# Two of three block sums of a MoE1 pair kept in PSUM instead of SBUF, with one relu-and-round step from there, and a schedule replanned around it

## The chip, the core and the metric

The kernel runs on one core of a Trainium2 chip. The core has TensorE (PE, matmuls, with PEld for its weight loads), VectorE (DVE), ScalarE (ACT), GpSimd (POOL) and SyncE (SP, which here only issues DMAs). Matmuls write to PSUM, eight banks of 128 partitions x 512 fp32; the other operands lie in SBUF. The metric is the device time of one execution in microseconds (us), the median of several runs.

## The reference

Chunked attention (4 batches x 8 heads x 576 tokens, chunks of 64), then a mixture of four experts with relu (MoE1), then a gated feed-forward layer (MoE2), all in fp32:

```python
scores = scale * np.matmul(q_c, k_c.transpose(0, 1, 2, 4, 3))     # inside chunks of 64
attn = softmax(scores); x = np.matmul(attn, v_c)                  # -> x: (2304, 512)
for e in range(4):                                                # MoE1, w1 (512, 1024), w2 (1024, 512)
    out += p[:, e:e + 1] * (np.maximum(x @ w1[e], 0.0) @ w2[e])
h = out @ w_in                                                    # MoE2, w_in (512, 2048), w_out (2048, 512)
g = h * np.clip(h + 3.0, 0.0, 6.0) / 6.0
return g @ w_out
```

## The kernel before

**Tiling.** The 2304 tokens go through in three sets of 768, each set as two halves `z` of N = 384 tokens. A layer runs in groups of 512 hidden columns: eight groups `g` in MoE1 (`ph` 0) and four in MoE2 (`ph` 1). The program order of the matmuls is all of MoE1 for the three sets, then all of MoE2. A group has an **h part** (x times the first weight matrix, line L881, or L928 for the first group of each MoE1 set) and a **y part** (72 matmuls of 512 columns, L977, which multiply the activated h with the second weight matrix). Every fp32 operand is split in a rounded high part and a low part (`fp32r`), and each product is three matmuls (`HL`).

**The pair.** In all MoE1 groups but the first of each set, and in all of MoE2, the h part is computed by a scheme of seven products for a 2 x 2 block matrix (`h_pair`, called twice a group with `pr_` 0 and 1; MoE1 has 42 such pairs). The products run in the order P1, P6, P7, P5, P2, P4, P3, six matmuls of 384 columns each, into four PSUM banks of the tag `h`, called `a`, `b`, `c` and `d`: P1 and then P2 add up in `a`, P6 goes to `b`, P7 and then P4 to `c`, P5 and then P3 to `d`. VectorE forms the block sums with L891:

- `u2` = `b` + a copy of P1 (the copy is ScalarE's L898), into an SBUF tile `U`;
- `u3` = `c` + `U`, into an SBUF tile `V`; P4 waits for it, because it overwrites the bank's sum;
- `c22` = `d` + `V`, back into `V`; P3 waits for it;
- `c21` = `c` + `U` after P4, into a third SBUF tile `C`;
- `c12` = `d` + `U` after P3, back into `U`.

The fourth block, c11, is complete in bank `a` after P2.

**The gate.** Each of the four blocks then goes through `gate`, which must leave max(x, 0) as a rounded high part and a low part in a tile `gt`. For a block in PSUM (in MoE1: c11, and the plain first groups) that is two steps: ScalarE takes relu and rounds in one instruction (L951), VectorE makes max(x, 0) minus the high part (L952, its inputs one PSUM bank and one SBUF tile). For a block in SBUF (tag `c`: c22, c21 and c12) it is three: ScalarE takes relu in place (L947), ScalarE rounds (L948), VectorE subtracts (L949, both inputs in SBUF).

**PSUM.** Four banks have the tag `h`, three `y`, one `a`. The y part needs all three `y` banks. Attention of the next set is worked in between the matmuls of MoE1 in small steps (`Item`: transposes L535, scores L472, values L544), which take the `y` and `a` banks while TensorE is in an h part, and the `h` and `a` banks while it is in a y part. Its softmax runs on VectorE (L496, L501, L512, L513) and ScalarE (L505). VectorE's L512 waits for the last exponential of L505.

**What sets the order.** `Plan` lists every operation with an engine, a planned duration, a due time, its inputs and the buffers it takes, runs that list once in the kernel's own planning and then emits the instructions of every engine in the planned order. An engine takes its instructions strictly in that order, and waits where an input or a buffer is not there yet. The constants at the top (`SLACK`, `ITEMS`, `STAGES`, `LEAD`, `LOAD`, `CALM`) shift due times: of the attention steps (`ITEMS`), of the conversion of MoE2's weights, which arrive as 64-bit numbers and are converted on ScalarE, VectorE and GpSimd during MoE1 (`STAGES`), and of the weight transfers (`LEAD`, `LOAD`, `SLACK`). GpSimd splits weights (L716, L742, L825, L828) and issues the weight reloads (L767, L770).

Of the kernel before, what the change touches and what calls it, by code (L numbers as in the profile page):

```python
# [13 lines left out]
ALU = mybir.AluOpType  # L14
# [17 lines left out]
BANKS = (("hhhhh", "yahay"), ("ayaay", "yyyay"), ("ayaay", "ayaay"))
# [2 lines left out]
def raw(ap):  # L35
    return ap.bitcast(F32)
# [23 lines left out]
class Plan:  # L60
# [3 lines left out]
    LAT = 0.2  # L64
    EVERY = 0.6
    DENSE = 7.77
    CALM = 6.53
    LANES = 8

    def __init__(self, caps, filler=None, warm=0.0):  # L70
# [164 lines left out]
def fused_kernel(ctx: ExitStack, tc: tile.TileContext, q, k, v, probs, w1, w2, win, wout, out):  # L235
    nc = tc.nc
    B, H, S, D = q.shape
# [60 lines left out]
    op = plan.op  # L298
# [37 lines left out]
    for u in units:  # L336
        ph, si, g, c0, n = u
# [528 lines left out]
    def h_pair(u, pr_):  # L866
# [31 lines left out]
        cp = op("ACT", act(n), lambda: nc.scalar.copy(S(p1)(), a_()), e(0), [o["P1"]], [p1], [ps["a"]])  # L898
        u2 = op("DVE", dve(n), add(S(U), b_, S(p1)), e(1), [o["P6"], cp], [U], [ps["b"], p1])
        u3 = op("DVE", dve(n), add(S(V), c_, S(U)), e(2), [o["P7"], u2], [V], [ps["c"], U])  # L900
        c22 = op("DVE", dve(n), add(S(V), d_, S(V)), e(3), [o["P5"], u3], (), [ps["d"], V])
        product("P2", [cp])
        product("P4", [u3])
        product("P3", [c22])
        C = buf("c")
        gate(u, 2 + pr_, 1, S(V), [V], [c22], e(3, 0.5))
        gate(u, 0 + pr_, 0, a_, [ps["a"]], [o["P2"]], e(4, 0.1))
        c21 = op("DVE", dve(n), add(S(C), c_, S(U)), e(5), [o["P4"], u2], [C], [ps["c"], U])
        gate(u, 2 + pr_, 0, S(C), [C], [c21], e(5, 0.5))
        c12 = op("DVE", dve(n), add(S(U), d_, S(U)), e(6), [o["P3"], c21, u3], (), [ps["d"], U])  # L910
        gate(u, 0 + pr_, 1, S(U), [U], [c12], e(6, 0.5))

    HL = ((0, 0), (0, 1), (1, 0))

# [26 lines left out]
    def gate(u, f, z, src, bufs, after, due, n=N):  # L941
        ph, si, g, _, _ = u
        due -= soon(u)
        G = buf("gt")
        hi_, lo_ = (lambda: G.t[:, 0, :n]), (lambda: G.t[:, 1, :n])
        if ph == 0 and bufs[0].tag == "c":
            x = op("ACT", act(n), lambda: nc.scalar.activation(src(), src(), AF.Relu), due, after, (), bufs)  # L947
            hi = op("ACT", act(n), lambda: nc.scalar.copy(hi_(), src()), due + 0.1, [x], [G], bufs)  # L948
            lo = op("DVE", dve(n) * busy(ph), lambda: nc.vector.tensor_tensor(out=lo_(), in0=src(), in1=raw(hi_()), op=ALU.subtract), due + 0.3, [hi], (), [G, *bufs])  # L949
        elif ph == 0:  # L950
            hi = op("ACT", act(n), lambda: nc.scalar.activation(hi_(), src(), AF.Relu), due, after, [G], bufs)  # L951
            lo = op("DVE", dve(n), lambda: nc.vector.scalar_tensor_tensor(out=lo_(), in0=src(), scalar=0.0, in1=raw(hi_()), op0=ALU.max, op1=ALU.subtract), due + 0.3, [hi, *after], (), [G, *bufs])  # L952
        else:
            R = buf("t")
            r_ = lambda: R.t[:, :n]
            x = op("ACT", act(n), lambda: nc.scalar.activation(r_(), src(), AF.Relu, bias=half, scale=1.0 / 6.0), due, after, [R], bufs)  # L956
            x = op("DVE", dve(n), lambda: nc.vector.scalar_tensor_tensor(out=r_(), in0=r_(), scalar=1.0, in1=src(), op0=ALU.min, op1=ALU.mult), due + 0.3, [x, *after], (), [R, *bufs])  # L957
            hi = op("ACT", act(n), lambda: nc.scalar.copy(hi_(), r_()), due + 0.6, [x], [G], [R])  # L958
            lo = op("DVE", dve(n), lambda: nc.vector.tensor_tensor(out=lo_(), in0=r_(), in1=raw(hi_()), op=ALU.subtract), due + 0.9, [hi], (), [G, R])  # L959
        gts[u, f, z] = (G, lo, 0)  # L960
        return G, lo
# [239 lines left out]
```

## Time and profile before

| | |
|---|---|
| median of 3 runs (lowest, highest) | 1197.85 us (1197.01, 1198.44) |
| profiled execution, its own time | 1196.41 us |
| span of its trace | 1194.4 us |
| TensorE busy | 1175.8 us (98%) |
| VectorE, ScalarE, GpSimd busy | 731.8, 512.4, 497.2 us |
| granted TensorE clock | full in every slice of the span |

The span is the time from the first to the last instruction of the trace; the profiled execution's own time is 2.0 us longer. An engine's busy time counts its instructions, not its waits. TensorE's matmuls are pipelined, so its idle time is what is to be looked at here: the moments in which it had no matmul in flight, and what ended each of them.

### The profile page before, as it was taken

What the parts mean: (1) busy time and instruction counts of PE and PEld (TensorE: products, weight loads), DVE (VectorE), ACT (ScalarE), POOL (GpSimd) and SP (SyncE); (2) the same over time, 40 slices, a digit from 0 to 9 for tenths busy, and PEclk for the clock granted to TensorE, in tenths of its full rate; (3) what the DMA queues carried; (4) which work ended last, traced back from release to release, by engine and by line L of the source; (5) the groups of instructions that cost most, each with busy time, mean ns of one, the idle gap of its engine ahead of it and who ended that gap; (6) DMA issues with size and microseconds to landing.
All of it is one profiled execution on the core that took longest, in us unless ns stands there. A gap on an engine that the chain in (4) does not pass through costs nothing.

```text
span 1194.4 us, 19308 instructions
## 1 busy us (share of the span) xinstructions
PE 1175.8 (98%) x7028; PEld 1057.8 (89%) x7028; DVE 731.8 (61%) x1318; ACT 512.4 (43%) x1208; POOL 497.2 (42%) x569
## 2 busy tenths in 40 slices
PE   8999999999999999999999999999999999999998
PEld 7898988889989898878989999999999999989997
DVE  5656555557574776568647655758455845583555
ACT  6764545544355443444343434333323442244222
POOL 3686665641354554664365566531111111111110
PEclk9999999999999999999999999999999999999999
DMA  9788978758779997887788878966955885576651
GB/s 249 291 282 305 301 266 290 274 195 255 207 216 328 293 299 234 287 275 238 225 279 294 283 255 288 337 208 198 267 180 182 238 233 182 189 247 194 194 177 53
DMA packets 147470, 292.29 MB, mean 245 GB/s; under 512 B 69808, under 2 KB 76208, under 8 KB 147376
## 3 DMA queue, kind: packets, MB, share of 16 engines
q0 software_dynamic: 43488, 158.35, 41.7%
q1 hardware_dynamic: 102144, 131.01, 34.3%
q10 hardware_dynamic: 1744, 1.70, 0.5%
q8 instruction: 55, 0.90, 0.3%
q14 instruction: 39, 0.32, 0.1%
HBM read 213.95 MB, written 77.07 MB: 244 GB/s over the span
## 4 chain that ended last, share of the span: by engine, by line
PE 92%; DVE 3%; issue 3%; POOL 2%; DMA 1%; ACT 0%; DVEq 0%; POOLq 0%; ACTq 0%
PE y L977 47%; PE h L881 37%; PE h L928 4%; DMA k<-wp 1%; DVE c L891 1%; PE y L295 0%; POOL wp L716 0%; PE a L535 0%; DVE gt L949 0%; POOL t L742 0%; PE y L454 0%; PE h L472 0%; PE h L544 0%; PE y L544 0%; DVE wh L716 0%
## 5 line engine op out<-in xcount | busy, mean ns | idle before, releaser
L977 PE MATMUL y<-wy,gt 128*128 128x512 f32 x2592 | 602.6, 391 | 0.8 <-DVE acc L1013 0.8
L977 PEld LDWEIGHTS y<-wy,gt 128*128 128x128 f32 x2592 | 484.3, 188 | 100.4 <-DVE acc L1013 1.2
L881 PE MATMUL h<-x,wh 128*128 128x384 f32 x2772 | 492.6, 336 | 6.9 <-DVE c L891 6.5
L881 PEld LDWEIGHTS h<-x,wh 128*128 128x128 f32 x2772 | 481.1, 188 | 13.1 <-DVE c L891 9.5
L767 POOL DMA_DIRECT2D wh<-k x190 | 103.5, 546 | 210.5 <-PE h L881 181.8
L891 DVE TENSOR_TENSOR c<-h,c 128x384 f32<-128x384 f32 x264 | 145.8, 553 | 67.5 <-PE h L881 64.1
L770 POOL DMA_DIRECT2D wy<-k x112 | 61.0, 545 | 266.0 <-PE y L977 260.3
L1013 DVE SCALAR_TENSOR_TENSOR acc<-y,pn,acc 128x512 f32<-128x512 f32 x126 | 89.0, 751 | 131.2 <-PE y L977 131.2
L949 DVE TENSOR_TENSOR gt<-c,gt 128x384 fp32r<-128x384 f32 x126 | 111.0, 887 | 8.6 <-ACT gt L948 8.4
L947 ACT ACTIVATE c<-c 128x384 f32<-128x384 f32 x126 | 65.3, 525 | 101.2 <-DVE c L891 101.0
L891 DVE TENSOR_TENSOR c<-h,p 128x384 f32<-128x384 f32 x66 | 36.7, 556 | 102.5 <-PE h L881 87.6
L898 ACT COPY p<-h 128x384 f32<-128x384 f32 x66 | 31.6, 479 | 153.6 <-PE h L881 153.6
L1020 DVE TENSOR_TENSOR acc<-y,acc 128x512 f32<-128x512 f32 x53 | 36.3, 692 | 65.2 <-PE y L977 65.2
L948 ACT CAST gt<-c 128x384 fp32r<-128x384 f32 x126 | 63.4, 511 | 2.1
L956 ACT ACTIVATE t<-c,half 128x384 f32<-128x384 f32 x72 | 43.1, 613 | 38.9 <-DVE c L891 38.9
L958 ACT CAST gt<-t 128x384 fp32r<-128x384 f32 x96 | 47.0, 513 | 27.4 <-DVE t L957 27.4
L928 PE MATMUL h<-x,wh 128*128 128x384 f32 (+1 forms) x336 | 53.2, 315 | 1.0 <-DVE x L692 1.0
L928 PEld LDWEIGHTS h<-x,wh 128*128 128x128 f32 x336 | 51.4, 189 | 1.7 <-DVE x L692 1.2
L716 POOL TENSOR_TENSOR wy<-t,wy 128x512 fp32r<-128x512 f32 x32 | 41.1, 1291 | 28.0 <-ACT wy L714 25.7
L716 POOL TENSOR_TENSOR wp<-t,wp 128x512 fp32r<-128x512 f32 x32 | 41.7, 1306 | 24.6 <-ACT wp L714 24.2
L959 DVE TENSOR_TENSOR gt<-t,gt 128x384 fp32r<-128x384 f32 x96 | 50.0, 551 | 1.0
L655 ACT CAST x<-xs 128x768 fp32r<-128x768 f32 x33 | 27.0, 833 | 45.2 <-DVE xs L662 39.5
(140 smaller groups left out, 995.6 us busy)
## 6 DMA issues: line engine op xcount, KB each, us to landing
wh<-k POOLq DMA_DIRECT2D x190, 512.0 KB, 6.1
wy<-k POOLq DMA_DIRECT2D x112, 512.0 KB, 4.7
k<-wh SPq DMA_DIRECT2D x53, 512.0 KB, 3.5
k<-wp SPq DMA_DIRECT2D x44, 512.0 KB, 5.6
k<-wy SPq DMA_DIRECT2D x32, 512.0 KB, 4.6
t<-in_moe_w_dram SPq DMA_DIRECT2D x32, 256.0 KB, 4.9
w<-in_moe_w_in_dram SPq DMA_DIRECT2D x16, 512.0 KB, 5.4
w<-in_moe_w_out_dram SPq DMA_DIRECT2D x16, 512.0 KB, 5.8
```

Source lines behind the costliest of these rows:

```text
L716: return op(eng, gps(512) if eng == "POOL" else dve(512), lambda: e.tensor_tensor(out=view(b.t[:, 1]), in0=read(), in1=raw(view(b.t[:, 0]) ...
L767: wready[at_] = op("POOL", 0.6, lambda b=b, name=name: nc.gpsimd.dma_start(out=b.t, in_=kept[ph, g, name]), t - LEAD[0] + j, [stored[ph, g ...
L770: wready[key, "y", f] = op("POOL", 0.6, lambda b=b, f=f: nc.gpsimd.dma_start(out=b.t, in_=kept[ph, g, f]), t_y - LEAD[3] + n_, [stored[ph, ...
L881: nc.tensor.matmul(acc.t[:, :n], W.t[:, a, k_ * 256 + pr_ * P:k_ * 256 + (pr_ + 1) * P], X.t[:, b, k_, cs], start=new and first, stop=last ...
L891: add = lambda out, x, y: (lambda: nc.vector.tensor_tensor(out=out(), in0=x(), in1=y(), op=ALU.add))
L928: nc.tensor.matmul(ps.t[:, :m], Ws[k_ // 2].t[:, a, k_ % 2 * 256 + f % 2 * P:k_ % 2 * 256 + f % 2 * P + P], x if len(zs) == 2 else x[:, zs ...
L947: x = op("ACT", act(n), lambda: nc.scalar.activation(src(), src(), AF.Relu), due, after, (), bufs)
L948: hi = op("ACT", act(n), lambda: nc.scalar.copy(hi_(), src()), due + 0.1, [x], [G], bufs)
L949: lo = op("DVE", dve(n) * busy(ph), lambda: nc.vector.tensor_tensor(out=lo_(), in0=src(), in1=raw(hi_()), op=ALU.subtract), due + 0.3, [hi ...
L959: lo = op("DVE", dve(n), lambda: nc.vector.tensor_tensor(out=lo_(), in0=r_(), in1=raw(hi_()), op=ALU.subtract), due + 0.9, [hi], (), [G, R])
L977: nc.tensor.matmul(ps[j].t, G.t[:, a, o + j * P:o + (j + 1) * P], W.t[:, b, :], start=f == FO[0] and i == 0, stop=f == FO[-1] and i == len ...
L1013: fn = lambda: nc.vector.scalar_tensor_tensor(out=A.t, in0=ps.t, scalar=p, in1=A.t, op0=ALU.mult, op1=ALU.add)
```

## The change

Two of the three sums of a MoE1 pair no longer go to an SBUF tile. For each pair a table `BACK` says where c22, c21 and c12 are written: `p` is the PSUM bank that already took part in the sum (`b` for c22, `c` for c21), `y` a PSUM bank of the tag `y`, `s` SBUF as before. With `("pys", "pps")`, c22 goes to bank `b` in both pairs, c21 to a `y` bank in the first pair of a group and back into bank `c` in the second, and c12 stays in SBUF. Since `gate` looks at where the block lies, c22 and c21 now take its two-step way (ScalarE relu and rounding, VectorE low part). MoE2 is written as before. The planned duration of the low part that remains in SBUF is set to 0.81, and the constants of the plan are other numbers, so the whole order of MoE1 is planned anew.

```diff
-SLACK = (6.22, 4.56, 3.86, 0.88)
+SLACK = (6.85, 4.4, 5.78, 0.84)
...
-ITEMS = (48.78, 11.34, -32.4, 5.76)
-STAGES = (26.1, -30.31)
-LEAD = (12.76, 24.57, 7.4, 8.63)
-LOAD = 15.86
+ITEMS = (50.1, 19.22, -34.0, 4.11)
+STAGES = (22.53, -48.06)
+LEAD = (15.26, 27.02, 8.22, 8.26)
+LOAD = 16.23
+BACK = ("pys", "pps")
+LO = 0.81
...
-    CALM = 6.53
+    CALM = 6.55
...
-        c22 = op("DVE", dve(n), add(S(V), d_, S(V)), e(3), [o["P5"], u3], (), [ps["d"], V])
+
+
+        def goal(k_, own, there):
+            way = BACK[pr_][k_] if ph == 0 else "s"
+            if way == "p":
+                return own, []
+            if way == "s" and there is not None:
+                return there, []
+            b = buf("c" if way == "s" else "y")
+            return b, [b]
+        at22, n22 = goal(0, ps["b"], V)
+        at21, n21 = goal(1, ps["c"], None)
+        at12, n12 = goal(2, ps["d"], U)
+        c22 = op("DVE", dve(n), add(S(at22), d_, S(V)), e(3), [o["P5"], u2, u3], n22, [ps["d"], V, at22])
...
-        C = buf("c")
-        gate(u, 2 + pr_, 1, S(V), [V], [c22], e(3, 0.5))
+        gate(u, 2 + pr_, 1, S(at22), [at22], [c22], e(3, 0.5))
         gate(u, 0 + pr_, 0, a_, [ps["a"]], [o["P2"]], e(4, 0.1))
-        c21 = op("DVE", dve(n), add(S(C), c_, S(U)), e(5), [o["P4"], u2], [C], [ps["c"], U])
-        gate(u, 2 + pr_, 0, S(C), [C], [c21], e(5, 0.5))
-        c12 = op("DVE", dve(n), add(S(U), d_, S(U)), e(6), [o["P3"], c21, u3], (), [ps["d"], U])
-        gate(u, 0 + pr_, 1, S(U), [U], [c12], e(6, 0.5))
+        c21 = op("DVE", dve(n), add(S(at21), c_, S(U)), e(5), [o["P4"], u2], n21, [ps["c"], U, at21])
+        gate(u, 2 + pr_, 0, S(at21), [at21], [c21], e(5, 0.5))
+        c12 = op("DVE", dve(n), add(S(at12), d_, S(U)), e(6), [o["P3"], c21, c22, u3], n12, [ps["d"], U, at12])
+        gate(u, 0 + pr_, 1, S(at12), [at12], [c12], e(6, 0.5))
...
-            lo = op("DVE", dve(n) * busy(ph), lambda: nc.vector.tensor_tensor(out=lo_(), in0=src(), in1=raw(hi_()), op=ALU.subtract), due + 0.3, [hi], (), [G, *bufs])
+            lo = op("DVE", LO, lambda: nc.vector.tensor_tensor(out=lo_(), in0=src(), in1=raw(hi_()), op=ALU.subtract), due + 0.3, [hi], (), [G, *bufs])
```

In the pieces below the rows of the changed kernel carry its own line numbers: L893 is the block sums (L891 before), L966 the low part from PSUM (L952), L963 the low part from SBUF (L949), L961 and L962 ScalarE's two steps (L947, L948), L965 its one step (L951), and L467, L498, L503, L514 and L515 the attention's transposes and softmax steps (L465, L496, L501, L512, L513). The order of TensorE up to the end of the first h part by pairs is the same in both kernels.

**First place: VectorE in the second pair of the first paired group of the second set**, about 341 to 350 us of the trace. `c` is an SBUF tile, `h` a PSUM bank, `gt` the gate's output. Before:

```order
L949 TENSOR_TENSOR gt_4206<-c_4106,gt_4206 128x384
L891 TENSOR_TENSOR c_4218<-h_4211,c_4218 128x384
L465 STREAM_TRANSPOSE tri_78<-kr_4020 128x192
L891 TENSOR_TENSOR c_4260<-h_4193,c_4204 128x384
L949 TENSOR_TENSOR gt_4252<-c_4218,gt_4252 128x384
L952 SCALAR_TENSOR_TENSOR gt_4262<-h_4157,gt_4262 128x384
L891 TENSOR_TENSOR c_4204<-h_4211,c_4204 128x384
L949 TENSOR_TENSOR gt_4273<-c_4260,gt_4273 128x384
```

The same stretch in the changed kernel:

```order
L963 TENSOR_TENSOR gt_4169<-c_4071,gt_4169 128x384
L893 TENSOR_TENSOR c_4192<-h_4149,c_4167 128x384
L467 STREAM_TRANSPOSE tri_78<-kr_3990 128x192
L893 TENSOR_TENSOR h_4132<-h_4171,c_4192 128x384
L893 TENSOR_TENSOR h_4149<-h_4149,c_4167 128x384
L966 SCALAR_TENSOR_TENSOR gt_4203<-h_4132,gt_4203 128x384
L966 SCALAR_TENSOR_TENSOR gt_4223<-h_4123,gt_4223 128x384
L966 SCALAR_TENSOR_TENSOR gt_4228<-h_4149,gt_4228 128x384
L893 TENSOR_TENSOR c_4167<-h_4171,c_4167 128x384
```

The low parts of c22 and c21 read a PSUM bank now and stand ahead of the sum c12; the low part of the first pair's c12 (the first row of both pieces) still reads SBUF, and stands ahead of `u3` now (the second row) where it stood behind it.

**Second place: VectorE in the first pair of the fifth paired group of the first set**, about 203 to 208 us of the trace, where an attention step lies inside the h part. Before:

```order
L891 TENSOR_TENSOR c_2773<-h_2750,c_2743 128x384
L465 STREAM_TRANSPOSE tri_78<-qr_2588 128x6x32
L891 TENSOR_TENSOR c_2773<-h_2765,c_2773 128x384
L465 STREAM_TRANSPOSE tri_78<-kr_2605 128x192
L512 TENSOR_TENSOR st_2775<-st_2775,least_62 128x6
L513 RECIPROCAL st_2775<-st_2775 128x6
L465 STREAM_TRANSPOSE tri_78<-kr_2605 128x192
L891 TENSOR_TENSOR c_2824<-h_2750,c_2743 128x384
L949 TENSOR_TENSOR gt_2807<-c_2773,gt_2807 128x384
L952 SCALAR_TENSOR_TENSOR gt_2822<-h_2685,gt_2822 128x384
```

And in the changed kernel:

```order
L893 TENSOR_TENSOR c_2753<-h_2727,c_2719 128x384
L467 STREAM_TRANSPOSE tri_78<-qr_2568 128x6x32
L893 TENSOR_TENSOR h_2677<-h_2746,c_2753 128x384
L467 STREAM_TRANSPOSE tri_78<-kr_2586 128x192
L514 TENSOR_TENSOR st_2755<-st_2755,least_62 128x6
L515 RECIPROCAL st_2755<-st_2755 128x6
L467 STREAM_TRANSPOSE tri_78<-kr_2586 128x192
L966 SCALAR_TENSOR_TENSOR gt_2784<-h_2677,gt_2784 128x384
L966 SCALAR_TENSOR_TENSOR gt_2788<-h_2666,gt_2788 128x384
L893 TENSOR_TENSOR y_2812<-h_2727,c_2719 128x384
```

c22 now lies in bank `b` (`h_2677`), which stays taken until its low part, the eighth row, has read it; c21 goes to a `y` bank.

**Third place: ScalarE in the pair of the first place.** Before:

```order
L947 ACTIVATE c_4106<-c_4106 128x384
L714 CAST wp_4200<-rh_3825 128x512
L948 CAST gt_4206<-c_4106 128x384
L947 ACTIVATE c_4218<-c_4218 128x384
L948 CAST gt_4252<-c_4218 128x384
L951 ACTIVATE gt_4262<-h_4157 128x384
L947 ACTIVATE c_4260<-c_4260 128x384
L948 CAST gt_4273<-c_4260 128x384
```

And in the changed kernel:

```order
L716 CAST wp_4144<-rh_3791 128x512
L961 ACTIVATE c_4071<-c_4071 128x384
L962 CAST gt_4169<-c_4071 128x384
L965 ACTIVATE gt_4203<-h_4132 128x384
L965 ACTIVATE gt_4223<-h_4123 128x384
L965 ACTIVATE gt_4228<-h_4149 128x384
```

The two instructions of c22 and of c21 have become one each.

## Rows read from the trace of the kernel before

**Rows 1.** The page's engines: busy us (share of the span) x instructions.

```profile
PE 1175.8 (98%) x7028; PEld 1057.8 (89%) x7028; DVE 731.8 (61%) x1318; ACT 512.4 (43%) x1208; POOL 497.2 (42%) x569
```

**Rows 2.** Stretches: length, busy by engine (PE, PEld, DVE, ACT, POOL), clock, DMA share, GB/s.

```profile
0.00:66.00 66.00, 61.13 (x728) 54.24 (x729) 41.68 (x84) 46.39 (x125) 33.97 (x34) 1.00 0.86 264
66.00:650.00 584.00, 574.14 (x3589) 514.71 (x3588) 366.92 (x661) 272.30 (x714) 315.29 (x318) 1.00 0.82 266
650.00:1140.00 490.00, 490.00 (x2468) 444.30 (x2467) 295.75 (x523) 180.39 (x345) 144.24 (x212) 1.00 0.74 231
```

**Rows 3.** TensorE's waits from 66 to 650 us: total us, times, longest.

```profile
PE h L881 <- DVE c L891: 6.5, 7, 1.8
PE h L472 <- DVE gt L952: 2.2, 1, 2.2
```

**Rows 4.** Groups by line and shape: busy us, mean ns of one, idle before.

```profile
L891 DVE TENSOR_TENSOR c<-h,c 128x384 f32<-128x384 f32 x264 | 145.8, 553 | 67.5 <-PE h L881 64.1
L949 DVE TENSOR_TENSOR gt<-c,gt 128x384 fp32r<-128x384 f32 x126 | 111.0, 887 | 8.6 <-ACT gt L948 8.4
L947 ACT ACTIVATE c<-c 128x384 f32<-128x384 f32 x126 | 65.3, 525 | 101.2 <-DVE c L891 101.0
L948 ACT CAST gt<-c 128x384 fp32r<-128x384 f32 x126 | 63.4, 511 | 2.1
L952 DVE SCALAR_TENSOR_TENSOR gt<-h,gt 128x384 fp32r<-128x384 f32 x58 | 31.9, 550 | 8.5 <-ACT gt L951 8.5
L951 ACT ACTIVATE gt<-h 128x384 fp32r<-128x384 f32 x58 | 28.3, 488 | 26.2 <-PE h L928 26.0
```

**Rows 5.** The low parts line by line: ns shortest/median/longest, first and last start us.

```profile
L949 DVE TENSOR_TENSOR gt<-c,gt x126: 510/558/4062, 72.9 to 806.4; 128x384 fp32r<-128x384 f32 x126
L952 DVE SCALAR_TENSOR_TENSOR gt<-h,gt x70: 410/549/558, 29.6 to 803.3; 128x384 fp32r<-128x384 f32 x58, 128x256 fp32r<-128x256 f32 x12
L959 DVE TENSOR_TENSOR gt<-t,gt x96: 519/551/561, 825.8 to 1177.4; 128x384 fp32r<-128x384 f32 x96
```

**Rows 6.** Timeline, 344 to 350 us (start us, us): VectorE, then the TensorE step.

```profile
344.59 4.06 DVE L949 TENSOR_TENSOR gt<-c,gt 128x384 fp32r<-128x384 f32 x1
348.58 0.55 DVE L952 SCALAR_TENSOR_TENSOR gt<-h,gt 128x384 fp32r<-128x384 f32 x1
...
349.18 0.27 PE L472 MATMUL h<-tri 64*64 64x64 f32 x2 [2.16 <-DVE gt L952]
```

**Rows 7.** Timeline: VectorE's long low parts, and TensorE's waits behind them.

```profile
511.67 2.12 DVE L949 TENSOR_TENSOR gt<-c,gt 128x384 fp32r<-128x384 f32 x2
...
514.98 1.34 PE L881 MATMUL h<-x,wh 128*128 128x384 f32 x6 [1.84 <-DVE c L891]
...
546.22 1.56 DVE L949 TENSOR_TENSOR gt<-c,gt 128x384 fp32r<-128x384 f32 x1
...
548.50 0.79 PE L881 MATMUL h<-x,wh 128*128 128x384 f32 x3 [1.57 <-DVE c L891]
...
611.20 3.43 DVE L949 TENSOR_TENSOR gt<-c,gt 128x384 fp32r<-128x384 f32 x1
...
615.15 0.44 PE L881 MATMUL h<-x,wh 128*128 128x384 f32 x1 [1.34 <-DVE c L891]
```

**Rows 8.** Timeline of the second place: VectorE's L512 and c21, TensorE's matmuls.

```profile
205.70 0.17 DVE L512 TENSOR_TENSOR st<-st,least 128x6 f32<-128x6 f32 x1 [0.60 <-ACT e L505]
...
206.26 0.52 DVE L891 TENSOR_TENSOR c<-h,c 128x384 f32<-128x384 f32 x1
...
201.52 7.56 PE L881 MATMUL h<-x,wh 128*128 128x384 f32 x42
```

**Rows 9.** An undisturbed pair: TensorE's start, VectorE's c22; and an h part's length.

```profile
600.10 13.71 PE L881 MATMUL h<-x,wh 128*128 128x384 f32 x78
...
604.48 0.56 DVE L891 TENSOR_TENSOR c<-h,c 128x384 f32<-128x384 f32 x1 [0.48 <-PE h L881]
...
663.77 14.58 PE h L881 x84
```

## The prediction

> **What bounds the kernel now.** I read the page's engines first: TensorE is busy for 1175.8 of 1194.4 us, 98% [rows 1]. So the kernel is bound by its matmuls, and no change beside them can gain more than the 18.6 us in which TensorE stands still. Next I read the stretches, to see where those 18.6 us lie [rows 2]. From 0 to 66 us there are 66.00 - 61.13 = 4.9 us, in the start, where TensorE's order is the same in both kernels. From 650 to 1140 us, the last MoE1 groups and nearly all of MoE2, there is nothing: 490.00 of 490.00. The rest after 1140 us is the end of the program. What is left is MoE1 from 66 to 650 us: 584.00 - 574.14 = 9.9 us. [...] These 9.9 us are all that the change can take back.
>
> Then I read who ends TensorE's waits in that stretch [rows 3]. Seven waits, 6.5 us, are matmuls of the h part that wait for a block sum on VectorE (L891); one of 2.2 us is an attention step that waits for a low part (L952). No wait is ended by a DMA. Yet VectorE is busy for only 366.92 of the 584 us [rows 2]. It is not short of time, it is late in single places. The groups and the spread of single durations tell why [rows 4, 5]. The low part from SBUF (L949) has a median of 558 ns but a mean of 887 and a longest of 4062. The low part from PSUM (L952) never takes over 558. L949's long ones stand straight ahead of TensorE's waits: 4.06 us at 344.59, and c11's L952, which the attention step waits for, starts when it is over [rows 6]; 2.12 for two, 1.56 and 3.43 us, with waits of 1.84, 1.57 and 1.34 us behind them [rows 7]. MoE2's subtraction from two SBUF tiles (L959) stays within 561 ns [rows 5]; it stands in a stretch where GpSimd is busy for 144.24 of 490 us, against 315.29 of 584 in MoE1 [rows 2]. So my reading is that a VectorE instruction with both inputs in SBUF is held while GpSimd works on SBUF, and one with an input in PSUM is not.
>
> **The change part by part.** *Removed on ScalarE:* for c22 and c21 of 42 pairs, 84 gates, 525 + 511 ns become one step of 488 ns (L951) [rows 4]: 84 x 0.548 = 46 us of ScalarE time. All of it lies beside TensorE's work; its worth is that a low part can start 0.5 us sooner.
>
> *Removed on VectorE:* 84 x (887 - 550) ns = 28 us [rows 4], beside TensorE's work too, except where a wait stands behind it. I go through those waits. The step at 349.18 waited 2.16 us for the c22 low part of 4.06; that part now reads PSUM: 2.2 us go. At 546.22 the low part is c21's; 1.56 becomes 0.55, so 1.0 of 1.57 us goes. At 511.67 the first of two is c21's and the second c12's, which stays in SBUF and can be held in its place; I take half of 1.84, 0.9. At 611.20 it is c12's: nothing goes. What is left of 9.9 us is 9.9 - 2.2 - 1.84 - 1.57 - 1.34 = 3.0 us of smaller waits; two of three low parts are relieved there, but other VectorE work of two SBUF inputs stands in them too, so I take 1.2. Sum: 2.2 + 1.0 + 0.9 + 1.2 = 5.3 us gone.
>
> *Added: block sums written to PSUM.* No VectorE instruction of the trace writes PSUM. The nearest row is the same sum written to SBUF, 553 ns [rows 4]; a gain can't be excluded, down to the 510 ns that the shortest L949 took, and the dearest instruction of this width is L949's mean, 887 ns [rows 4, 5]. I take 553, since the work is the same and one input was in PSUM before. At 887 it would cost 0.33 us in each pair, which the margin below hides except in the seven tight pairs: 2.3 us at most.
>
> *Added: banks held longer.* This is the price of the change. Before, bank `b` was free once `u2` had read it; now it is taken until c22's low part has read it, and the second pair's first product waits for a bank. Undisturbed, c22 starts 4.38 us after its pair (604.48 - 600.10) and a pair lasts 14.58 / 2 = 7.29 us [rows 9]. Sum, relu and low part take 0.553 + 0.488 + 0.550 = 1.6 us [rows 4], so the bank is free at some 6.0 to 6.1, 1.2 us early. But VectorE works in order, and where an attention step lies in the h part, the softmax's L512 stands ahead of that low part (the second place), and it waits for ScalarE's exponentials (0.60 us) [rows 8]. The low part would stand where c21 stands now, at 206.26, and end at 206.81; the second pair's matmuls start 5 products after 201.52, at 201.52 + 30 x 14.58 / 84 = 206.73 [rows 8, 9]. That is a wait of 0.1 to 0.2 us. I count seven first pairs with those softmax steps ahead of c22's low part: 7 x 0.15 = 1.0 us.
>
> *Moved.* The attention steps inside the y part stand nine matmuls behind its start instead of six in most groups, because they need all four `h` banks; that moves them and costs no TensorE time. The weight conversion for MoE2 ends some 14 us sooner against its start (-48.06 + 30.31, with the start 3.57 earlier), so GpSimd's 315 us lie a few in a hundred denser; what hides it is VectorE's slack, and if that is gone it is c12's low part that pays. The DMA issues on SP and POOL change places by a few rows each; they cost nothing as long as no wait of TensorE is ended by a DMA, as now [rows 3]. c12's low part stands ahead of `u3` in about half of the second pairs: `u3` can start at about 3.3 us and P4 needs it at 5 x 1.04 = 5.2, so such a low part may last about 1.8 us before TensorE waits; behind `u3` it delays c22 instead, with the same room. This is the same exposure as at 611.20, for 42 low parts instead of 126.
>
> [...] Rows first: reading the block from PSUM costs VectorE nothing, 549 ns at the median against 551 from SBUF [rows 5]. [...]
>
> *Sum.* The profiled execution took 1196.41 us, 2.0 us more than its span, and 1.44 us less than the median of the runs, 1197.85. 1196.41 - 5.3 + 1.0 = 1192.1; with the 1.44 us back to the median, **1193.5 us**.
>
> **The rivals.** *Nearly all waits go* (to 1190.5 and below). If relieving VectorE lets c12's low parts and the rest fall into gaps, up to 9.9 us go: 1196.41 - 9.9 + 1.44 = 1188.0. For it: MoE2, whose L959 are never held, has no TensorE wait at all [rows 2]. Against: 611.20 is untouched by the change.
>
> *The held time moves to c12* (no measurable change). 42 low parts from SBUF remain, GpSimd's work is denser, and one held for 3.43 us cost 1.34 us [rows 7]. Two or three more such, 2.7 to 4.0 us, beside the 1.0 us for the banks leave 0.3 to 1.6 us of the 5.3: 1196.2 to 1197.6. For it: L949's long ones come by chance of what GpSimd runs at that moment, and a new order draws anew. Against: TensorE waited behind few of 126.
>
> *The banks decide* (slower). If ScalarE is late with the relu of c22, behind a weight cast or the exponentials, the second pair's first product waits in all 21 groups, and not in seven pairs. It decides from 1.2 us of other work ahead of that chain; at 0.4 us in each of the 21 it costs 8.4 us: 1197.85 - 5.3 + 8.4 = 1201. For it: VectorE's L512 already waits for ScalarE. Against: ScalarE is busy for 272.30 of 584 us [rows 2] and loses 46 us.
>
> That the change does not do what it says can be left out: its VectorE order has 42 low parts from SBUF, and the 84 others read a bank.
>
> **How the numbers follow.** My forecast, 1190.5 to 1195.4, has 0.47; nearly all gone 0.15; no change 0.26; slower 0.12. A measurement of this kernel can tell about 0.2%, 2.4 us. So faster (below 1195.45) has 0.62, same (1195.45 to 1200.25) 0.26, slower 0.12. The range goes from 1188.0, where all waits are gone, to 1199.5, which takes in no change, the dearest PSUM write (1193.5 + 2.3) and the weak end of the third rival; what it leaves out are the rest of that rival and whatever goes below.
>
> **What would show it.** Right: L949's successor is seen 42 times, the low parts from PSUM 154 times with none over 0.6 us; ScalarE's busy time falls by about 46 us and VectorE's by about 28; TensorE idles for 5 to 6 us in the same stretch; what is left of its waits stands behind c12's low part or a softmax step. Wrong: block sums that write PSUM at clearly over 0.6 us; TensorE's first product of second pairs waiting for a low part in most groups; waits ended by a DMA; or TensorE's busy time itself moving.

## The result, and the profile after

The changed kernel takes 1186.18 us (median of 4 runs, 1185.55 to 1186.75), the kernel before 1197.82 (4 runs, 1197.01 to 1198.44). The ratio is 0.9903, with a 95% interval of 0.9886 to 0.992. That is 11.6 us, 1.0%, faster. The sign was forecast; the size was not: 1186.18 lies 7.3 us below the forecast of 1193.5, below the range (1188.0 to 1199.5) and below the rival "nearly all waits go" (1188.0). The profiled run took 1185.55 us with a span of 1183.8.

The first lines are the page's engines and the same three stretches as in [rows 1, 2]; the last is the only row left of those that [rows 3] came from: TensorE's waits from 66 to 650 us (total us, times, longest).

```profile
PE 1172.9 (99%) x7028; PEld 1056.8 (89%) x7028; DVE 698.1 (59%) x1318; ACT 474.3 (40%) x1124; POOL 492.8 (42%) x569
...
0.00:66.00 66.00, 60.66 (x730) 53.54 (x731) 42.08 (x84) 46.60 (x126) 34.16 (x35) 1.00 0.88 264
66.00:650.00 584.00, 582.78 (x3639) 523.99 (x3638) 341.49 (x669) 246.24 (x653) 316.72 (x322) 1.00 0.84 272
650.00:1140.00 490.00, 490.00 (x2471) 444.44 (x2470) 294.19 (x528) 172.41 (x328) 139.81 (x210) 1.00 0.73 229
...
PE h L883 <- DVE h L893: 1.2, 1, 1.2
```

TensorE now idles for 584.00 - 582.78 = 1.22 us in the stretch where it idled for 9.86 [rows 2], and that is one wait. The rest of the stretch runs without a gap. But two things changed on TensorE: its idle time, 18.6 us of the span before and 1183.8 - 1172.9 = 10.9 now, and its *busy* time, 1175.8 before [rows 1] and 1172.9 now, with the same 7028 matmuls. 7.7 us of the span's 10.6 are idle time, 2.9 are busy time.

Next the low parts and block sums line by line (ns shortest/median/longest, first and last start), to set beside [rows 5]. L963 is the old L949 (both inputs in SBUF), L966 the old L952 (one input in PSUM), L893 the old L891 (block sums; `h` and `y` are PSUM, `c` is SBUF).

```profile
L963 DVE TENSOR_TENSOR gt<-c,gt x42: 516/553/3299, 76.8 to 795.3; 128x384 fp32r<-128x384 f32 x42
...
L966 DVE SCALAR_TENSOR_TENSOR gt<-h,gt x133: 410/548/559, 29.3 to 792.6; 128x384 fp32r<-128x384 f32 x121, 128x256 fp32r<-128x256 f32 x12
L966 DVE SCALAR_TENSOR_TENSOR gt<-y,gt x21: 546/548/559, 73.7 to 784.6; 128x384 fp32r<-128x384 f32 x21
...
L893 DVE TENSOR_TENSOR c<-h,c x180: 544/557/560, 69.1 to 1163.3; 128x384 f32<-128x384 f32 x180
L893 DVE TENSOR_TENSOR h<-h,c x63: 532/566/567, 70.1 to 790.3; 128x384 f32<-128x384 f32 x63
L893 DVE TENSOR_TENSOR y<-h,c x21: 550/566/567, 72.2 to 783.0; 128x384 f32<-128x384 f32 x21
```

All 154 low parts from PSUM end within 559 ns. The 42 from SBUF (c12's) still reach 3299. A block sum written to PSUM takes 566 ns at the median, 9 more than one written to SBUF.

The one wait that is left is the place that the prediction left untouched, 611.20 in [rows 7], now at 600. These are VectorE, GpSimd and TensorE there in the timeline (start us, us).

```profile
598.76 3.81 PE L883 MATMUL h<-x,wh 128*128 128x384 f32 x21
...
599.95 3.30 DVE L963 TENSOR_TENSOR gt<-c,gt 128x384 fp32r<-128x384 f32 x1
600.30 1.29 POOL L744 TENSOR_TENSOR t<-rh,t 128x512 f32<-128x512 f32 x1
601.54 1.28 POOL L718 TENSOR_TENSOR wp<-t,wp 128x512 fp32r<-128x512 f32 x1
...
603.17 0.55 DVE L893 TENSOR_TENSOR h<-h,c 128x384 f32<-128x384 f32 x1
...
603.78 1.32 PE L883 MATMUL h<-x,wh 128*128 128x384 f32 x6 [1.22 <-DVE h L893]
```

c12's low part stands on VectorE from 599.95 to 603.25, some 0.4 us behind the end of GpSimd's two instructions (601.54 + 1.28 = 602.82); the next block sum stands behind it, and TensorE waits 1.22 us for that sum. The rows also show a cost that the wait's own number leaves out. Six matmuls after the wait take 1.32 us until their last one ends, and the 21 before it 3.81 us, where 84 in a row take 14.58 [rows 9], 0.174 each: 6 x 0.174 = 1.04 and 21 x 0.174 = 3.65. The stream that stops runs out (0.16 us more) and starts again slowly (0.28 us from the first start to the second, 0.17 otherwise); both are counted as busy. (In the kernel before, the last matmul ahead of the wait runs 0.16 us over in nine of its ten waits.)

### The profile page after: what moved, and what is told of

Same layout as the page of the kernel before. It is cut to its first block, busy times and chain, and to the rows that moved or that the text cites. A ratio compares the mean times of both kernels' runs of the same rounds, so it can differ in the third digit from the quotient of the medians.

```text
span 1183.8 us, 19222 instructions
## 1 busy us (share of the span) xinstructions
PE 1172.9 (99%) x7028; PEld 1056.8 (89%) x7028; DVE 698.1 (59%) x1318; ACT 474.3 (40%) x1124; POOL 492.8 (42%) x569
## 4 chain that ended last, share of the span: by engine, by line
PE 98%; DVE 1%; DMA 0%; issue 0%; ACT 0%; DVEq 0%
PE y L991 50%; PE h L883 41%; PE h L942 4%; PE a L537 1%; PE y L546 0%; DMA kr<-in_k_dram 0%; PE y L456 0%; PE h L546 0%; PE y L474 0%; PE h L474 0%; DVE wh L718 0%; PE a L546 0%; PE a L474 0%; DVE x L694 0%; DVE st L498 0%
## 5 line engine op out<-in xcount | busy, mean ns | idle before, releaser
L991 PE MATMUL y<-wy,gt 128*128 128x512 f32 x2592 | 600.8, 391 | 0.0
L991 PEld LDWEIGHTS y<-wy,gt 128*128 128x128 f32 x2592 | 484.3, 188 | 99.7 <-DVE gt L966 0.2
L883 PE MATMUL h<-x,wh 128*128 128x384 f32 x2772 | 492.0, 335 | 1.2 <-DVE h L893 1.2
L883 PEld LDWEIGHTS h<-x,wh 128*128 128x128 f32 x2772 | 481.2, 188 | 5.5 <-DVE h L893 2.1
L1027 DVE SCALAR_TENSOR_TENSOR acc<-y,pn,acc 128x512 f32<-128x512 f32 x126 | 89.1, 751 | 142.9 <-PE y L991 142.7
L893 DVE TENSOR_TENSOR c<-h,c 128x384 f32<-128x384 f32 x180 | 99.8, 554 | 26.5 <-PE h L883 22.7
L965 ACT ACTIVATE gt<-h 128x384 fp32r<-128x384 f32 (+1 forms) x133 | 60.8, 484 | 107.0 <-DVE h L893 74.0
L893 DVE TENSOR_TENSOR c<-h,p 128x384 f32<-128x384 f32 x66 | 36.7, 557 | 106.6 <-PE h L883 95.7
L966 DVE SCALAR_TENSOR_TENSOR gt<-h,gt 128x384 fp32r<-128x384 f32 (+1 forms) x133 | 67.4, 538 | 20.1 <-ACT gt L965 19.9
L716 ACT CAST wp<-t 128x512 fp32r<-128x512 f32 x32 | 19.9, 622 | 82.0 <-POOL t L830 52.6
L893 DVE TENSOR_TENSOR h<-h,c 128x384 f32<-128x384 f32 x63 | 35.4, 563 | 22.1 <-PE h L883 20.7
```

What stands on the lines that cost most here:

```text
L883: nc.tensor.matmul(acc.t[:, :n], W.t[:, a, k_ * 256 + pr_ * P:k_ * 256 + (pr_ + 1) * P], X.t[:, b, k_, cs], start=new and first, stop=last ...
L893: add = lambda out, x, y: (lambda: nc.vector.tensor_tensor(out=out(), in0=x(), in1=y(), op=ALU.add))
L991: nc.tensor.matmul(ps[j].t, G.t[:, a, o + j * P:o + (j + 1) * P], W.t[:, b, :], start=f == FO[0] and i == 0, stop=f == FO[-1] and i == len ...
L1027: fn = lambda: nc.vector.scalar_tensor_tensor(out=A.t, in0=ps.t, scalar=p, in1=A.t, op0=ALU.mult, op1=ALU.add)
```

## The experiments

The theory: VectorE's instructions with two SBUF inputs are held while GpSimd works on SBUF, and a few long ones, ahead of a sum that TensorE needs, make the loss. Its rivals: the new plan numbers (SLACK, ITEMS, STAGES, LEAD, LOAD, CALM, LO) give the gain by another order; or ScalarE's shorter chain gives it. The kernel before, run beside them, took 1197.15 (first four), 1197.52 (next four) and 1197.3 us (last four).

**e1_psum_old: the sums in PSUM, the plan's old numbers.**

```diff
-SLACK = (6.85, 4.4, 5.78, 0.84)
+SLACK = (6.22, 4.56, 3.86, 0.88)
...
-LO = 0.81
+LO = 0.728
```

(and ITEMS, STAGES, LEAD, LOAD, CALM as before)

> The sums c22 and c21 in PSUM as in the changed kernel, but with the plan's old numbers (SLACK, ITEMS, STAGES, LEAD, LOAD, CALM, and 0.728 for the low part from SBUF). Theory A (VectorE is no longer held, wherever the plan puts things): most of the 11.6 us stay, 1186 to 1190, TensorE's idle time from 66 to 650 us at most 3 us. Theory B (the new plan did it): 1194 to 1198, idle 6 to 10 us.

Measured: 1189.06 us (1187.71 to 1189.66), ratio 0.9929 (0.9913 to 0.9946). So 8.1 us come without the new numbers, as the first theory expected. The waits from 66 to 650 us, and the timeline at the longer one (ScalarE, VectorE, TensorE):

```profile
PE h L883 <- DVE gt L966: 2.3, 1, 2.3
PE h L883 <- DVE h L893: 0.6, 1, 0.6
...
370.10 0.62 ACT L716 CAST wp<-rh 128x512 fp32r<-128x512 f32 x1 [3.18 <-DMA k<-wp]
370.62 0.86 ACT L965 ACTIVATE gt<-h 128x384 fp32r<-128x384 f32 x2
371.14 1.02 DVE L966 SCALAR_TENSOR_TENSOR gt<-h,gt 128x384 fp32r<-128x384 f32 x2 [2.90 <-ACT gt L965]
...
371.75 1.33 PE L883 MATMUL h<-x,wh 128*128 128x384 f32 x6 [2.26 <-DVE gt L966]
```

This is the prediction's third rival (the banks), at one place: ScalarE's weight cast waits 3.18 us for a DMA, the two relus stand behind it, the low parts behind them, and TensorE cannot have the bank for the second pair's first product. With the new numbers the place is free of it.

**e2_sbuf_new: all sums in SBUF, the new numbers.**

```diff
-BACK = ("pys", "pps")
+BACK = ("sss", "sss")
```

> All three sums in SBUF as before the change, but with the plan's new numbers. Theory A: 1194 to 1200, the 126 low parts at 0.8 to 0.9 us in the mean, idle 7 to 12 us. Theory B: 1186 to 1190, though the low parts are held as before.

Measured: 1200.7 us (1200.36 to 1202.08), ratio 1.003 (1.0019 to 1.0041). The new numbers alone cost 3.5 us, a little more than expected (1194 to 1200, and 800 to 900 ns for the mean low part, which took 940). The low parts from SBUF (ns shortest/median/longest), the waits from 66 to 650 us, the place at 484 us, and one stretch behind it:

```profile
L963 DVE TENSOR_TENSOR gt<-c,gt x126: 514/558/8174, 72.8 to 810.9; 128x384 fp32r<-128x384 f32 x126
...
PE y L991 <- DVE gt L963: 4.6, 1, 4.6
PE h L474 <- DVE gt L966: 4.1, 1, 4.1
...
484.56 8.64 DVE L963 TENSOR_TENSOR gt<-c,gt 128x384 fp32r<-128x384 f32 x2
...
491.50 0.82 POOL L533 TENSOR_TENSOR e<-e,st 128x384 f32<-128x384 f32 x1
...
492.79 6.59 PE L991 MATMUL y<-wy,gt 128*128 128x512 f32 x19 [4.58 <-DVE gt L963]
...
492.50:497.00 4.50, 4.21 (x10) 3.34 (x11) 3.24 (x6) 0.00 (x0) 0.00 (x0) 0.50 0.00 1
```

Two low parts last 8.64 us. The first alone takes 8.17 (the longest of the 126), until the last of seven GpSimd instructions in a row is over (491.50 + 0.82 = 492.32); the second then runs. Behind the wait TensorE's granted clock is 0.50, from 492.5 to 497.0 us, and 19 matmuls take 6.59 us.

**e3_sbuf_two: as e2, with relu and rounding in one step there too** (so that the low part computes relu itself, from two SBUF inputs).

```diff
-        if ph == 0 and bufs[0].tag == "c":
+        if False:
```

> Sums in SBUF, new numbers, but all gates in two steps: ScalarE relu and rounding in one instruction from SBUF, VectorE max and subtraction in one, with both inputs in SBUF. It has the shorter ScalarE chain without PSUM. Theory A (holding): the low parts stay at 0.8 us or more in the mean, time 1193 to 1199. Theory C (one ScalarE step less, so earlier low parts): 1186 to 1190.

Measured: 1194.73 us (1192.02 to 1196.26), ratio 0.9976 (0.9966 to 0.9987). The group of the low parts, the longest row of TensorE's waits, and its longest wait in the timeline:

```profile
L966 DVE SCALAR_TENSOR_TENSOR gt<-c,gt 128x384 fp32r<-128x384 f32 x126 | 108.5, 867 | 19.0 <-ACT gt L965 18.5
...
PE h L883 <- DVE c L893: 5.4, 2, 4.4
...
379.12 0.62 ACT L716 CAST wp<-t 128x512 fp32r<-128x512 f32 x1 [4.76 <-DMA k<-wp]
...
380.20 1.30 DVE L966 SCALAR_TENSOR_TENSOR gt<-c,gt 128x384 fp32r<-128x384 f32 x1 [4.34 <-ACT gt L965]
...
382.03 1.33 PE L883 MATMUL h<-x,wh 128*128 128x384 f32 x3 [4.37 <-DVE c L893]
```

The fused form is held like the plain one (mean 867 ns with both inputs in SBUF, 549 with one in PSUM): here it is the inputs' place, not the operation. But the time of e3 does not speak against the rival of ScalarE's shorter chain. Of its 7.4 us of idle time, 4.4 and 1.2 us stand behind weight casts on ScalarE that wait for a DMA; behind held low parts there is under 1 us (0.75 us of the 4.4, and a wait of 0.2). With 40 us still held, the two-step gates, or the order that came with them, took most of the waits behind held low parts away, and e3 is 6.0 us faster than e2. What speaks against that rival as the cause is e4 and e8.

**e4_psum_three: the changed kernel with relu and rounding in two steps again.**

```diff
-        if ph == 0 and bufs[0].tag == "c":
+        if ph == 0 and (bufs[0].tag == "c" or f >= 2 and not is_plain(u)):
```

> Sums in PSUM, new numbers, but c22 and c21 go through three steps: relu in place in PSUM, rounding, subtraction from PSUM. It has VectorE's relief without ScalarE's. Theory A: 1186 to 1189, low parts from PSUM at 0.55 us, none over 0.6. Theory C: 1192 to 1198; it also holds bank b longer by one ScalarE step of about 0.5 us, which the 1.2 us margin should bear.

Measured: 1189.68 us (1188.31 to 1190.35), ratio 0.9931 (0.9916 to 0.9946). The plain subtraction, by the place of its input:

```profile
L963 DVE TENSOR_TENSOR gt<-h,gt x63: 520/548/559, 73.5 to 797.1; 128x384 fp32r<-128x384 f32 x63
L963 DVE TENSOR_TENSOR gt<-c,gt x42: 519/553/3861, 77.7 to 798.5; 128x384 fp32r<-128x384 f32 x42
```

The same line, operation and shape stays within 559 ns with an input in PSUM and reaches 3861 with both in SBUF. The low parts came as the first theory expected, the time 0.7 us above its 1186 to 1189. ScalarE's second step costs up to 3.5 us here; since the order moves with it, not all of that need be the step itself.

**e5_c22 and e6_c21: only one of the two sums in PSUM, new numbers** (`BACK = ("pss", "pss")` and `("sys", "sps")`).

> Only c22 in PSUM (bank b, both pairs), c21 and c12 in SBUF, the plan's new numbers. c22's low part stands at the end of an h part, where an attention step or the next matmuls wait behind it; c21's stands inside the next pair, ahead of u3 or c22. If each held low part costs alike, half way between the 1200.7 us with all sums in SBUF and the 1186.2 us of the changed kernel: 1192 to 1195. If the waits come mainly from c22's low part, 1187 to 1190.

> Only c21 in PSUM (a y bank in the first pair, bank c in the second), c22 and c12 in SBUF, the plan's new numbers. If each held low part costs alike: 1192 to 1195. If the waits come mainly from c22's: 1195 to 1200.

Measured: e5_c22 1199.05 us (1196.19 to 1202.82), ratio 1.0011 (0.9998 to 1.0024); e6_c21 1197.31 (1196.38 to 1198.84), ratio 1.0 (0.9991 to 1.001). Neither gains half, so the expectation that each held low part costs alike missed. e6 lies where it was to lie if c22's low part made the waits (1195 to 1200), but e5, which relieves c22's, does not (1187 to 1190). e5's place at 482 us in the timeline, and e6's two waits:

```profile
482.43 3.28 DVE L963 TENSOR_TENSOR gt<-c,gt 128x384 fp32r<-128x384 f32 x1
...
485.63 0.55 DVE L893 TENSOR_TENSOR h<-h,c 128x384 f32<-128x384 f32 x1
...
486.24 1.32 PE L883 MATMUL h<-x,wh 128*128 128x384 f32 x6 [2.35 <-DVE h L893]
```

```profile
PE h L474 <- DVE gt L966: 4.5, 1, 4.5
PE h L546 <- DVE gt L966: 3.6, 1, 3.6
```

One third of the low parts was relieved. In e6 the others, held for 6.75 and 6.00 us, still decide: the two waits are 8.1 of 8.8 us. In e5 it is less plain. Some 4.4 of its 10.4 us stand behind held VectorE instructions (at 350, 482 and 562 us); 1.8 us stand behind a weight cast on ScalarE that waits 7.94 us for a DMA, and the rest behind a few VectorE and ScalarE instructions that come late.

**e7_all: c12 in PSUM too** (`BACK = ("pyp", "ppp")`).

> c12 in PSUM too (bank d, in place), the plan's new numbers. The changed kernel has one wait left, 1.22 us behind a c12 low part of 3.30 us from SBUF; that one goes. The second pair's last product then waits for bank d until c12's low part has read it, which needs 0.55 + 0.49 + 0.55 us after the last product. If the banks bear that: 1184.5 to 1186. If they don't: 1187 to 1192, with waits of TensorE that a low part ends.

Measured: 1194.97 us (1193.14 to 1197.41), ratio 0.9979 (0.9969 to 0.9988). No low part is held any more, and it is 8.8 us slower than the changed kernel, and slower than the expected 1187 to 1192. First, who ended the idle time ahead of L883's matmuls and weight loads (us, times); then a first pair's end at 377 us in the timeline:

```profile
  DVE gt L966: 14.6, 21
...
374.91 0.62 ACT L716 CAST wp<-rh 128x512 fp32r<-128x512 f32 x1 [2.50 <-DMA k<-wp]
...
377.26 0.50 ACT L965 ACTIVATE gt<-h 128x384 fp32r<-128x384 f32 x1
...
377.79 0.56 DVE L966 SCALAR_TENSOR_TENSOR gt<-h,gt 128x384 fp32r<-128x384 f32 x1
...
378.40 1.92 PE L883 MATMUL h<-x,wh 128*128 128x384 f32 x7 [2.03 <-DVE gt L966]
```

Bank `d` now holds c12 until its low part is done, and the second pair's fourth product, P5, the last of its products to take a bank, waits for it: counted through L883's matmuls, 42 a pair, all nine idle gaps from 66 to 650 us stand ahead of a P5 of a second pair. This is the third rival's mechanism, on the bank that the change leaves alone and on another product; the longest wait also has a weight cast ahead of it that waited 2.50 us for a DMA. Most of these waits are short: the view of waits shows four of them, 3.6 us together, but TensorE's busy time is 1179.2 us, 6.3 over the changed kernel's (among it a piece at a granted clock of 0.50, from 380 to 382 us, behind the wait of 2.03 us). The profiled execution took 1197.41 us, 2.4 over the median, so these figures show e7 at its worst.

**e8_before_memset and e9_sbuf_new_memset: GpSimd's weight arithmetic replaced by writes of zeros**, in the kernel before, and in e2.

```diff
-            nc.gpsimd.tensor_tensor(out=low(), in0=low(), in1=dst(), op=ALU.mult)
+            nc.gpsimd.memset(low(), 0.0)
```

(and so at the three other places where GpSimd computes on weights; the kernels leave out the low halves of MoE1's weights and the values of MoE2's)

> The kernel before, order unchanged, but GpSimd's additions, subtractions and multiplications for the weights are replaced by writing zeros over the same tile (so the MoE1 weights lose their low parts and the MoE2 weights their values): GpSimd writes SBUF and reads none there. If VectorE's instructions with two SBUF inputs are held by GpSimd's reading, the 126 low parts of L949 come down from 887 ns to about 555 in the mean, none over 1 us outside the attention steps, and TensorE idles at most 3 us from 66 to 650 us. [...]

> All three sums in SBUF and the new plan numbers, as in e2_sbuf_new (1200.7), and GpSimd's weight arithmetic replaced by writes of zeros, so that GpSimd reads nothing from SBUF there (the low halves of MoE1's weights and the values of MoE2's weights are left out, the instructions stay). If what e2 lost is VectorE held by GpSimd: no low part above 2 us, TensorE idle between 66 and 650 us at most 2 us, no stretch at half clock, 1182 to 1188. If the new numbers are themselves a worse order for sums in SBUF: the two waits above 4 us stay and the time stays above 1194.

Measured: e8 1183.05 us (one run), e9 1184.76 (1183.34 to 1185.84), ratio 0.9893 (0.988 to 0.9906). The low parts from SBUF in each, and e8's middle stretch:

```profile
L949 DVE TENSOR_TENSOR gt<-c,gt x126: 515/549/1372, 71.6 to 793.0; 128x384 fp32r<-128x384 f32 x126
...
66.00:650.00 584.00, 583.54 (x3640) 524.12 (x3639) 330.00 (x670) 275.49 (x719) 172.59 (x321) 1.00 0.84 272
```

```profile
L963 DVE TENSOR_TENSOR gt<-c,gt x126: 514/549/733, 72.2 to 795.5; 128x384 fp32r<-128x384 f32 x126
```

This shows the cause. e8 has the order of the kernel before, its three-step gates and all sums in SBUF; only GpSimd's instructions differ, and 9.86 us of idle time become 0.46. e9 is e2 with the same edit: 1200.7 become 1184.8, so the new numbers are no worse an order in themselves, they only meet GpSimd at worse moments. The times alone don't separate one thing: the writes of zeros are also shorter (GpSimd is busy for 172.59 us of the stretch against 315.29 [rows 2]), so less reading and less time came together. The single instructions do. Counted through the traces, with an overlap of over 0.1 us: in the kernel before, 60 of L949's 126 overlap an addition, subtraction or multiplication on GpSimd, and they take 1.19 us at the median and up to 4.06; none of the other 66 takes over 0.56. In e8, 28 overlap a write of zeros, and none of them takes over 0.56 us; e8's one long low part (1372 ns, at 502.90) overlaps an attention step, L531, which still reads SBUF (from 503.00). In the changed kernel 79 of the low parts from PSUM overlap GpSimd's arithmetic, and none takes over 0.56.

**e10_c12_second: c12 in PSUM in second pairs alone** (`BACK = ("pys", "ppp")`), to keep bank `d` free for the second pair.

> The changed kernel with c12 too in PSUM, but only in the second pair of two, where no pair follows that needs bank d at once; in the first pair c12 stays in SBUF. If what slowed e7_all is bank d, held by c12's low part while the second pair's first product waits for it: no wait of a first product of a second pair for a low part, 21 low parts are left that can be held, 1184 to 1187. If a sum in bank d costs in either place (the next unit's products wait instead): waits of L883 for L966 again, above 1189.

Measured: 1194.88 us (1192.72 to 1198.31), ratio 0.9984 (0.9974 to 0.9993). The time missed the first expectation (1184 to 1187); it is above 1189, as the second had it, but not by the second's waits. The waits on a low part are gone, and two others came, 3.04 and 3.18 us:

```profile
367.32 0.62 ACT L716 CAST wp<-t 128x512 fp32r<-128x512 f32 x1 [10.49 <-DMA k<-wp]
367.85 0.47 ACT L900 COPY p<-h 128x384 f32<-128x384 f32 x1
...
368.37 1.32 PE L883 MATMUL h<-x,wh 128*128 128x384 f32 x6 [3.04 <-ACT p L900]
...
481.63 5.42 DVE L503 TENSOR_TENSOR st<-st,minus 128x6 f32<-128x6 f32 x1
...
485.75 1.28 POOL L744 TENSOR_TENSOR t<-rh,t 128x512 f32<-128x512 f32 x1
...
490.14 2.07 PE L991 MATMUL y<-wy,gt 128*128 128x512 f32 x4 [3.18 <-DVE acc L1027]
```

The first is ScalarE's queue behind a late DMA. The second is the old mechanism on another instruction: the softmax's L503, six elements wide and with two SBUF inputs, is held for 5.42 us while GpSimd goes from one instruction to the next, until 485.75 + 1.28 = 487.03; L1027, which TensorE waits for, stands behind it on VectorE.

**e11_c22_old and e12_c21_old: one sum in PSUM, old numbers.**

> Only c22 in PSUM, with the old plan numbers. With both sums there the old numbers gave 1189.1, that is 8.4 off before. If the gain goes by the number of low parts that can be held (126 to 84 here, to 42 with both): about half, 1192 to 1194.5. If it goes by the few held ones that stand in front of a sum that TensorE waits for: no rule by number; within 1 us of before or of e1_psum_old, as those few are c12's and c21's or c22's.

> Only c21 in PSUM, with the old plan numbers. By number of low parts that can be held: 1192 to 1194.5, and this gain and that of e11_c22_old add up to 8 to 9 us. By the few that stand in front of a sum that is waited for: the two gains don't add up to that.

Measured: e11 1189.32 us (1188.76 to 1190.29), ratio 0.9934 (0.9919 to 0.9948); e12 1191.25 (1190.88 to 1191.65), ratio 0.9948 (0.9935 to 0.9961). That is 8.0 and 6.1 us; with both sums, e1, it is 8.1. The gains don't add up, as the second expectation had it, and e11, within 1 us of e1, does not give the half that the number of low parts would. e12's whole idle time but 0.3 us is one place:

```profile
475.97 6.73 DVE L963 TENSOR_TENSOR gt<-c,gt 128x384 fp32r<-128x384 f32 x1
...
483.23 0.27 PE L474 MATMUL h<-tri 64*64 64x64 f32 x2 [4.50 <-DVE gt L966]
```

All kernels in one table: the low parts from SBUF, the time for which they are held (their number times their mean less 550 ns), TensorE's idle time from 66 to 650 us, and the median of the runs. Held and idle time are those of the one profiled execution, which took 1.5 to 2.4 us more than the median in e3, e5, e6 and e7 and lies within 1.5 us of it elsewhere.

| kernel | from SBUF | held us | idle us | time us |
|---|---|---|---|---|
| before | 126 | 42 | 9.9 | 1197.8 |
| e2 SBUF, new numbers | 126 | 49 | 10.2 | 1200.7 |
| e3 the same, two steps | 126 | 40 | 7.4 | 1194.7 |
| e5 c22, new | 84 | 29 | 10.4 | 1199.1 |
| e6 c21, new | 84 | 32 | 8.8 | 1197.3 |
| e12 c21, old | 84 | 27 | 4.8 | 1191.3 |
| e11 c22, old | 84 | 28 | 3.3 | 1189.3 |
| e1 both, old | 42 | 6 | 2.8 | 1189.1 |
| e4 both, three steps | 42 | 13 | 1.1 | 1189.7 |
| **after** | 42 | 11 | 1.2 | 1186.2 |
| e10 c12 in second pairs | 21 | 7 | 6.2 | 1194.9 |
| e7 all three | 0 | 0 | 4.2 | 1195.0 |
| e9 e2, GpSimd writes only | 126 | 0 | 1.8 | 1184.8 |
| e8 before, GpSimd writes only | 126 | 1 | 0.5 | 1183.1 |

The time roughly follows the idle time, and the idle time does not follow the held time: with 27 to 29 us held it is 3.3 us (e11), 4.8 (e12) and 10.4 (e5). What the idle time leaves out is in part the clock. Behind a wait the granted clock was 0.50 in e2 (349 to 353.5 and 492.5 to 497 us), in e5 (389 to 392) and in e7 (380 to 382); stretches around waits have a mean of 0.56 and 0.62 in e6 (351 to 356, 490 to 497), 0.58 in e10 (490 to 494) and 0.73 in e12 (482 to 486), and e3's whole span has 0.998. The time lost there counts as busy: in e2 ten matmuls kept TensorE busy for 4.21 of the 4.50 us from 492.5. No version that computes everything beat the changed kernel.

## Where the prediction failed, and what it had right

The prediction had the mechanism and failed on the size: three terms of its sum, named below, kept the forecast 7.3 us too high.

**The cause: right.** TensorE waited for VectorE, and VectorE's low parts were held by GpSimd, with both inputs in SBUF and not with one in PSUM; e4 and e8 show it. In e4 the same subtraction reaches 3861 ns with both inputs in SBUF and 559 with one in PSUM. In e8 the 28 low parts that overlap a write of zeros stay within 0.56 us, and in e2 low parts beside arithmetic that reads SBUF reach 8.17 us.

**Reading from PSUM: right.** I took it to cost VectorE nothing. In the changed kernel the low part takes 548 ns at the median from PSUM and 553 from SBUF.

**The PSUM write: right.** 566 ns at the median where I took 553; the dear end, 887, did not come.

**ScalarE and VectorE: right in mechanism.** The steps come to 128.7 us before [rows 4] and, of the same kind, 22.1 + 21.6 for c12 and 66.6 for L965 after, less the 28.3 that L951 had: 46.7 us less against 46. The page's busy time fell by 38.1 only, since back-to-back steps overlap (in e1 two L965 in a row take 0.86 us, where one takes 0.49). VectorE's fell by 33.7 against 28.

**What fails is the size, at three terms.** The sum came to 4.3 us net, the two profiled spans differ by 10.6; these 6.3 us are what follows. (The other 1.0 of the 7.3 is 0.8 from the median: I put back 1.44 us, and the changed kernel's profiled execution lies only 0.63 below its own; the rest is the time outside the span.) First, *the idle time gone*: I took 5.3 of 9.9 us, 8.64 went. Of the 3.3 us between, 0.9 is the second half of the wait at 511.67 and 0.6 the rest of that at 546.22: I had kept what c12 or the part's own length might leave, and the new order left nothing, which no step of mine foresaw. 1.8 us are the smaller waits, of which I took 1.2 of 3.0: all went. The 1.34 us at 611.20 stayed, as 1.22. Second, *the banks*: I took 1.0 us for seven tight pairs; no matmul of the changed kernel from 66 to 650 us waits for a low part, so the 0.15 us in seven places did not come. e1 shows that the mechanism is there (2.26 us at one place), and e7 that it costs where the margin is gone (3.6 us in four waits); the new order had the margin. Third, and this broke the bound: *"These 9.9 us are all that the change can take back"* held TensorE's busy time for fixed. It fell by 2.9 us, the last of the prediction's own signs of being wrong. As the waits of these two kernels show it, a wait costs its own length and about 0.3 us more that are counted as busy (0.16 as the stream runs out; the next six end 0.28 late, of which 0.16 is the last one's own end). Ten waits before, one after: nine times 0.3 is 2.7 us. That the two agree is an estimate and no proof. The sums by line (1.8 of the 2.9 us in the y part's L991, 0.6 in L883) are no test of it: two y parts, from 80 and 247 us, lost the attention steps inside them, whose matmuls overlap the y part's, and their L991 fell from 17.10 to 16.52 us each. Against these, 0.9 us of idle time came in outside the stretch (4.87 to 5.34 us in the first 66 us [rows 2], and after 1140), which I had at nothing: 3.3 + 1.0 + 2.9 - 0.9 = 6.3, the whole difference.

**The rivals.** "Nearly all waits go" is what happened, and I gave it 0.15. I had read the one untouched wait as evidence against the other waits' going, and the evidence for it, MoE2 without a wait, as weak. "The held time moves to c12" was real as a danger: e6 lands there, and e5 and e10 in part, on low parts still in SBUF or on the softmax. "The banks decide" names a late ScalarE behind a weight cast, and that came too, with and without banks: in e1, e3, e5, e7, e9 and e10 a TensorE wait of 1.7 to 4.4 us stands behind a weight cast that waits for a DMA, between 365 and 388 us. In the changed kernel such casts wait as well, up to 9.59 us (at 388 us), with no wait of TensorE behind them. That the changed kernel escapes both is its order, and no part of the prediction's reasoning: the same numbers cost 3.5 us without PSUM, and give 2.9 us with it.

## What to carry to other kernels

Where an engine off the critical path is late in single places, look for instructions whose median and mean part company (558 and 887 ns here [rows 4, 5]), and ask what differs in their operands. Here it paid to move one operand out of SBUF, but only to a place that nobody waited for: with c12 in its bank too, e7 took 8.8 us more. A stall was worth more than its length in the waits, by an estimated 0.3 us each, since the stream that stopped and restarted paid again under "busy"; so the bound made of idle time alone was too low. And partial removal of a rare, long stall need not give a partial gain: e5 and e6, with a third of the low parts relieved, took 1199.05 and 1197.31 us, the time of the kernel before (1197.52), while e11, with the old numbers, had nearly all of e1's gain (1189.32 against 1189.06). Which few remain in front of an awaited result decided, so a change of order has to be timed with the stall taken out as well (e9) before it is called good or bad.

## What the runs showed of the hardware that was not expected

In e2 and in e10 a held VectorE instruction was not let in between GpSimd instructions that followed each other: it took 8.17 us in e2 and 5.42 for a six-element one in e10, where one GpSimd instruction takes 1.3 us. It ended only after the last of seven GpSimd instructions in e2 (at 492.32 us), and of five in e10 (487.03).

Two SBUF inputs are not the only case. The weight conversion's TENSOR_SCALAR instructions, which read one SBUF tile, were held too: in the kernel before, 14 of the 96 (L813, L816, L822) overlap GpSimd's arithmetic and take 1.03 us at the median, and none of the others takes over 0.50. L813 alone (ns shortest/median/longest):

```profile
L813 DVE TENSOR_SCALAR t<-t x32: 385/419/2077, 300.5 to 771.4; 128x512 f32<-128x512 f32 x32
```

TensorE's granted clock fell behind some waits. In e2, after 4.58 us of waiting, it was 0.50 from 492.5 to 497.0 us, and 19 matmuls took 6.59 us; at the 600.8 us for 2592 that L991 takes in the changed kernel they would take 4.4, so by this estimate the wait cost 2.2 us more than it shows. The length of the wait alone did not tell when: in e5 the clock was 0.50 from 389 to 392 us behind a wait of 1.79 us; in e10 it stayed at 1.00 from 368 to 375 us, behind the one of 3.04 us, and was 0.58 in the mean from 490 to 494, behind the one of 3.18.
